# No block, last waits in order of issue, w_phi loaded by features, the gate column by one transpose, x on two queues, a split x block, swapped banks: small edits to a linear-attention and GEGLU kernel

## The chip, the cores and the metric

One core of one Trainium2 chip. The metric is the device time of one execution in microseconds (us). Every profile read here shows the granted TensorE clock at 1.00. "Span" is the time from the first to the last recorded instruction of the core.

## The reference

```python
x = A_x                                            # 1 x 2048 x 640, bf16
g = sigmoid((x * gate_w).sum(-1, keepdims=True))
# A: linear attention, 32 heads of 20; feature map = softmax(+p), softmax(-p) of p = head @ w_phi
# (p enters only through exponentials, so wq @ blockdiag(w_phi) can be folded beforehand; same for wk)
a = attention(x, wqkv, w_phi) @ wo
b = (gelu(x @ w_gate) * (x @ w_up)) @ w_down       # F = 1728
return g * a + (1 - g) * b
```

## The kernel before

The kernel keeps everything in SBUF. It warms TensorE with seven matmuls of zeros, transposes the first 512 tokens of x on TensorE, and computes v for them while the other operands land. A tile of x is 128 tokens, so these are tiles 0 to 3, and a block is four tiles. The other x blocks, wk and wq come through transposing DMAs on SyncE's queue ("turns" below). wk and wq are then multiplied with the block-diagonal w_phi on TensorE ("folds"). From about 16 us on, an almost unbroken stream of matmuls runs to 294 us. Matmuls write into PSUM, which the kernel uses in numbered banks. These are the parts that the change touches:

```python
    def finish(self, eng):                     # last thing in the program, on SyncE
        for q in self.queues.values():
            for L in q["lanes"]:
                if L["count"] > 0:
                    eng.wait_ge(L["sem"], L["count"])
        for e in self.engs.values():
            if e["count"] > 0:
                eng.wait_ge(e["sem"], e["count"])

    def run(self):
        nc = self.nc
        self.alloc()
        with nc.Block() as blk:
            @blk.sync
            def _(sp):
                self.sc = _Sched(nc, {"sp": (nc.sync, 16), "act": (nc.scalar, 4), "pool": (nc.gpsimd, 2)})
                self.loads(); self.attention_state(); self.ffn()      # (three lines, joined here)
                self.sc.finish(sp)
    # ...
    # loads(): w_phi as 20 x 640 and the gate row on ScalarE's queue; on SyncE's queue:
        xload(0); xload(2)                     # tokens 0..511, two halves
        for kt in range(KD): vload(kt)         # wv
        xblock(1)                              # tokens 512..1023 turned: tiles 4 to 7
        wload(self.wkT, D, "wkT")              # wk turned
        wload(self.wqT, 0, "wqT")
        xblock(2); xblock(3)
    # ...
    def blockdiag(self, banks):                # between the v steps of the first block
        # 5 matmuls spread w_phi over the partitions, 5 more turn the gate row into a column,
        # then VectorE multiplies each with a 0/1 mask out of PSUM  (cut)
    # ...
        self.v_early(4, 6)                     # v of tile 4, banks 6 and 7
        self.v_early(5, 0)
        f(0, "k", (2, 3), "d")                 # fold 0 of wk
        f(1, "k", (4, 5), "a")
        self.v_early(6, 6)
    # ...
    # ffn(): PSUM bank pairs for gate and up
        pairs = [(6, 7), (0, 1)]               # the last query projection wrote bank 7
```

The softmax here doesn't subtract the row's maximum and nothing guards it: scores larger than these inputs give would overflow.

## Time and profile before

| | |
|---|---|
| device time, three runs at first | 299.22 us (299.12 to 299.34) |
| device time, all later runs of it (42, in four jobs) | mean 298.75 us (298.20 to 299.72) |
| span, mean of those 42 | 297.02 us |
| span of the profiled execution | 297.3 us |

The page of the profile, its first lines and the engines' shares of the chain of waits. Columns of the engine line: busy us, share of the span, number of instructions.

```profile
span 297.3 us, 4821 instructions
PE 292.5 (98%) x1913; PEld 170.3 (57%) x1913; DVE 162.6 (55%) x322; ACT 104.3 (35%) x183; POOL 28.0 (9%) x56
...
PE 93%; SPq 2%; DMA 2%; ACT 1%; issue 0%; ACTq 0%
```

TensorE does nearly everything, so only its stops and the two ends of the program are left to gain in. This is the timeline of TensorE's matmuls in the first 17 us (start us, duration us, engine, line, operation, tiles, count, and in brackets the idle time before it):

```profile
4.45 2.08 PE L285 MATMUL ps<-ident,xtok 128*128 128x128 bf16 x20
6.36 3.44 PE L369 MATMUL ps<-w,xT 128*128 128x480 bf16 x24
9.73 0.48 PE L305 MATMUL ps<-wphi_sb,esel 20*128 20x140 bf16 x5
10.05 0.26 PE L313 MATMUL ps<-one,gw_row 1*128 1x1 bf16 x5
10.25 2.35 PE L369 MATMUL ps<-w,xT 128*128 128x480 bf16 x16
12.44 2.88 PE L360 MATMUL ps<-w,xT 128*128 128x512 bf16 x20
15.63 0.80 PE L340 MATMUL ps<-BD,wkT 128*128 128x140 bf16 x12 [0.31 <-DMA wkT<-in_A_wqkv_dram]
16.27 1.52 PE L360 MATMUL ps<-w,xT 128*128 128x512 bf16 x10
```

The ten small matmuls take 0.52 us of the queue (9.73 to 10.25). At 15.63 TensorE has waited for the turned wk. From start to start, TensorE stood still 0.48 us (its last matmul started at 15.10 and holds the queue 0.055).

The same view where the feed-forward part begins.

```profile
83.92 1.24 PE L617 MATMUL ps<-xT,wg_sb 128*128 128x512 bf16 x5
85.36 1.24 PE L617 MATMUL ps<-xT,wu_sb 128*128 128x512 bf16 x5 [0.19 <-ACT Eq L511]
```

The end, from the views of single source lines (line, queue, instruction, count: shortest/median/longest ns, first and last start in us). SyncE's waits are L98 and L101, the exit of the block is L130:

```profile
L98 SPq EVENT_SEMAPHORE  x7: 17/28/902, 295.4 to 296.6; - x7
L101 SPq EVENT_SEMAPHORE  x4: 28/28/28, 296.7 to 296.9; - x4
...
L130 SPq COMPARE_BRANCH  x1: 41/41/41, 297.0 to 297.0; - x1
L130 SPq DRAIN  x1: 13/13/13, 297.1 to 297.1; - x1
L130 SPq EVENT_SEMAPHORE  x1: 17/17/17, 297.3 to 297.3; - x1
L130 ACTq EVENT_SEMAPHORE  x1: 17/17/17, 297.3 to 297.3; - x1
L130 DVEq EVENT_SEMAPHORE  x1: 21/21/21, 297.3 to 297.3; - x1
L130 PEldq EVENT_SEMAPHORE  x1: 51/51/51, 297.3 to 297.3; - x1
```

The 902 ns wait is the one for the last output, which landed at 296.47. Everything after it is bookkeeping: 0.88 us.

### The profile page before, as it was taken

Reading aid. Unit: us, or ns where it says so; the run is one execution under the profiler, and the core shown is the slowest. Engines: PE = TensorE matmul, PEld = TensorE weight load, DVE = VectorE, ACT = ScalarE, POOL = GpSimd, SP = SyncE. Lnnn points to the kernel's source line nnn. Section 1 sums busy time; section 2 is a strip of 40 time slices with the busy share of each in tenths; the row PEclk is TensorE's granted clock in tenths of the full one; section 3 lists DMA queues with packets and bytes.
Section 4 is the critical chain, followed back from the end, with each engine's and each line's share of the span. In section 5 each row is a group of like instructions: output and inputs, shape, how many; then the busy total and the mean of one; then the engine's idle time right before and its main releaser. Section 6 shows DMA issues by size and latency. Waiting matters only on the chain.

```text
span 297.3 us, 4821 instructions
## 1 busy us (share of the span) xinstructions
PE 292.5 (98%) x1913; PEld 170.3 (57%) x1913; DVE 162.6 (55%) x322; ACT 104.3 (35%) x183; POOL 28.0 (9%) x56
## 2 busy tenths in 40 slices
PE   8999999999999999999999999999999999999996
PEld 4566566555554455765554567654556765555673
DVE  1338999998876578600777700077770007777100
ACT  3357787666673221112222211222221122222112
POOL 7000000000000011110111100011110001111000
DMA  7999990000001304211011130101111010111101
GB/s 217 203 223 337 356 345 29 0 0 2 0 2 32 57 8 35 49 46 44 3 23 22 24 44 24 44 0 25 22 22 46 22 45 2 22 24 22 44 24 44
DMA packets 38178, 18.85 MB, mean 63 GB/s; under 512 B 30219, under 2 KB 37900, under 8 KB 38156
## 3 DMA queue, kind: packets, MB, share of 16 engines
q1 hardware_dynamic: 37504, 18.52, 24.9%
q8 instruction: 15, 0.25, 0.3%
q10 hardware_dynamic: 652, 0.03, 0.2%
q14 instruction: 7, 0.06, 0.1%
HBM read 9.04 MB, written 2.62 MB: 39 GB/s over the span
## 4 chain that ended last, share of the span: by engine, by line
PE 93%; SPq 2%; DMA 2%; ACT 1%; issue 0%; ACTq 0%
PE ps L617 37%; PE ps L716 19%; PE ps L360 12%; PE ps L722 7%; PE ps L505 7%; PE ps L653 4%; PE ps L453 3%; DMA wkT<-in_A_wqkv_dram 2%; PE ps L627 1%; SPq L229 1%; PE ps L340 1%; PE ps L695 1%; SPq L216 1%; ACT Eq L511 1%; ACT Ek L419 0%
## 5 line engine op out<-in xcount | busy, mean ns | idle before, releaser
L622 DVE TENSOR_TENSOR hT<-ps,gl 128x512 bf16<-128x512 f32 x52 | 35.7, 689 | 80.1 <-PE ps L617 80.0
L617 PE MATMUL ps<-xT,wu_sb 128*128 128x512 bf16 x260 | 64.6, 379 | 0.2 <-ACT Eq L511 0.2
L617 PE MATMUL ps<-xT,wg_sb 128*128 128x512 bf16 x260 | 64.6, 379 | 0.0
L620 ACT ACTIVATE gl<-ps 128x512 bf16<-128x512 f32 x52 | 31.1, 597 | 82.9 <-PE ps L617 80.6
L716 PE MATMUL ps<-wd_sb,hT 128*128 128x320 bf16 (+2 forms) x416 | 59.3, 299 | 0.0
L716 PEld LDWEIGHTS ps<-wd_sb,hT 128*128 128x128 bf16 x416 | 40.2, 98 | 16.8
L682 POOL TENSOR_TENSOR Og<-O,O 128x640 bf16<-128x640 bf16 x16 | 22.3, 1396 | 244.6 <-DVE O L680 244.6
L617 PEld LDWEIGHTS ps<-xT,wu_sb 128*128 128x128 bf16 x260 | 25.4, 98 | 31.1 <-issue 0.7
L360 PE MATMUL ps<-w,xT 128*128 128x512 bf16 (+3 forms) x240 | 40.9, 321 | 0.0
L617 PEld LDWEIGHTS ps<-xT,wg_sb 128*128 128x128 bf16 x260 | 24.9, 98 | 26.5
L732 ACT ACTIVATE outsb<-ps,Gm 128x640 bf16<-128x640 f32 (+2 forms) x17 | 13.0, 763 | 71.5 <-PE ps L722 71.5
L360 PEld LDWEIGHTS ps<-w,xT 128*128 128x128 bf16 x240 | 22.4, 97 | 18.2
L430 DVE TENSOR_REDUCE Dk<-Ek 128x64 f32<-128x1280 bf16 x16 | 23.7, 1481 | 3.2 <-ACT gcol L422 3.2
L439 DVE TENSOR_TENSOR Ek<-Ek,Dk 128x640 bf16<-128x640 bf16 x32 | 25.0, 822 | 0.6
L505 PE MATMUL ps<-xT,wq 128*128 128x512 bf16 x100 | 24.7, 379 | 0.3 <-ACT Eq L511 0.3
L680 DVE TENSOR_TENSOR O<-ps,RH 128x640 bf16<-128x640 f32 x32 | 24.8, 816 | 0.0
L722 PE MATMUL ps<-wo_sb,goT 128*128 128x320 bf16 (+2 forms) x160 | 24.6, 299 | 0.0
L511 ACT ACTIVATE Eq<-ps 128x512 bf16<-128x512 f32 x40 | 21.7, 604 | 4.0 <-PE ps L505 4.0
L419 ACT ACTIVATE Ek<-ps 128x640 bf16<-128x640 f32 x32 | 20.7, 702 | 3.5 <-PE ps L360 3.5
L722 PEld LDWEIGHTS ps<-wo_sb,goT 128*128 128x128 bf16 x160 | 15.1, 98 | 7.2 <-issue 1.3
L653 PEld LDWEIGHTS ps<-KV,Eq 128*128 128x128 bf16 x192 | 12.0, 98 | 3.6
L653 PE MATMUL ps<-KV,Eq 128*128 128x154 bf16 x192 | 13.7, 221 | 0.0
(66 smaller groups left out, 151.4 us busy)
## 6 DMA issues: line engine op xcount, KB each, us to landing
out_dram<-outsb SPq DMA_DIRECT2D x15, 160.0 KB, 1.8
wd_sb<-in_B_w_down_dram SPq DMA_DIRECT2D x1, 2080.0 KB, 12.6
wg_sb<-in_B_w_gate_dram SPq DMA_DIRECT2D x1, 1120.0 KB, 5.7
wu_sb<-in_B_w_up_dram SPq DMA_DIRECT2D x1, 1120.0 KB, 9.5
wg_sb<-in_B_w_gate_dram SPq DMA_DIRECT2D x1, 960.0 KB, 9.8
wu_sb<-in_B_w_up_dram SPq DMA_DIRECT2D x1, 960.0 KB, 10.1
w<-in_A_wqkv_dram SPq DMA_DIRECT2D x5, 160.0 KB, 4.0
wo_sb<-in_A_wo_dram SPq DMA_DIRECT2D x1, 800.0 KB, 9.8
```

The lines of the kernel that those rows point to most:

```text
L360: sc.op("pe", lambda e, kt=kt: e.matmul(self.bank(bank)[:, bcol:bcol + n], self.xT[:, kt, t * P:(t + 1) * P], self.w3[:, kt, c0:c0 + n], s ...
L430: sc.op("dve", lambda e: e.tensor_reduce(self.Dk[:, se, 0, :].rearrange("p (s h) -> p s h", h=H), self.Ek[:, se, :, :].rearrange("p s (h d ...
L439: sc.op("dve", lambda e, v=v, r=r: e.tensor_tensor(v, v, r, ALU.mult), reads=[("Rk", se)], writes=[("Ek", se, s)])
L505: sc.op("pe", lambda e, kt=kt: e.matmul(self.bank(bank), self.wq2[:, kt, i * P:(i + 1) * P], self.xT[:, kt, b * self.BT:(b + 1) * self.BT] ...
L511: sc.op("act", lambda e, s=s, scale=scale: e.activation(self.Eq[:, s, i, b * self.BT:(b + 1) * self.BT], self.bank(bank), AF.Exp, scale=sc ...
L617: sc.op("pe", lambda e, kt=kt, w=w, bk=bk: e.matmul(self.bank(bk), w[:, kt, c * P:(c + 1) * P], xs(kt), start=(kt == 0), stop=(kt == self. ...
L620: sc.op("act", lambda e: e.activation(self.gl[:, slot, :], self.bank(banks[0]), AF.Gelu_apprx_tanh), reads=[("ps", banks[0])], writes=[("g ...
L622: sc.op("dve", lambda e: e.tensor_tensor(self.hT[:, c, :], self.bank(banks[1]), self.gl[:, slot, :], ALU.mult), reads=[("ps", banks[1]), ( ...
L653: sc.op("pe", lambda e, s=s, i=i, n=n, o0=o0, k0=k0, bk=bk, r=r: e.matmul(self.bank(bk)[:, o0:o0 + n], self.Eq[:, s, i, t * P:(t + 1) * P] ...
L680: dve(lambda e, o=o, f=f, s=s: e.tensor_tensor(o, V[s][:, :, :, 0:DH], f, ALU.mult), rb + [key(6 + s)], [("O", s, sl)], guard=old)
L716: sc.op("pe", lambda e: e.matmul(self.bank(bk, w), self.hT[:, c, tt * P:(tt + 1) * P], self.wd_sb[:, c, w0:w0 + w], start=(c == 0 and not ...
L722: sc.op("pe", lambda e: e.matmul(self.bank(bk, w), self.goT[:, gs, k, :], self.wo_sb[:, k, w0:w0 + w], start=False, stop=(k == self.KD - 1 ...
```

## The change

The intent: take the bookkeeping off the end, the ten small matmuls and the two stops off TensorE, and bring wk earlier. The core of the diff, with some lines joined (initialisers, allocations, the later x blocks and the pool engine's selector are cut):

```diff
     def finish(self, eng):
-        for q in self.queues.values(): ...
         for e in self.engs.values():
             if e["count"] > 0:
-                eng.wait_ge(e["sem"], e["count"])
+                self._wait(eng, _Ev(e["sem"], e["count"]))
+        lanes = [L for q in self.queues.values() for L in q["lanes"] if L["count"] > 0]
+        for L in sorted(lanes, key=lambda L: L["last"]):      # in order of issue
+            self._wait(eng, _Ev(L["sem"], L["count"]))
@@ run
-        with nc.Block() as blk:
-            @blk.sync
-            def _(sp): ...
+        self.loads(); self.attention_state(); self.ffn()
+        self.sc.finish(nc.sync)
@@ loads
-        xload(0); xload(2)                    # both on SyncE's queue
+        xload("sp", 0)
+        xload("act", 2)
+        # w_phi as (h d) f -> 128 partitions x 5 x 20 on ScalarE's queue; the gate row into 5 rows of a
+        # zeroed 128 x 128 tile gz
-        xblock(1)
+        xturn(4, 2)
         wload(self.wkT, D, "wkT")
+        xturn(6, 2)
         wload(self.wqT, 0, "wqT")
@@ blockdiag
-        # ten matmuls into PSUM, then five products out of PSUM
+        for i in range(self.KD):              # five products, SBUF to SBUF
+            sc.op("dve", ... BD[:, i] = wphi_sb[:, i, :] (broadcast over heads) * mask[:, i])
+    def gate_column(self, b):
+        sc.op("pe", lambda e: e.transpose(pv, self.gz[:, :], self.ident[:, :]), ...)
+        sc.op("dve", lambda e: e.tensor_copy(self.w3[:, :, 2*D:2*D+1], pv[:, 0:KD].unsqueeze(2)), ...)
@@ attention_state
-        vs(0, 0); vs(1, 0); vs(2, 0); vs(0, 1); vs(3, 0); ...
+        for t in range(4): vs(t, 0)           # plain order
@@ ffn
-        pairs = [(6, 7), (0, 1)]
+        pairs = [(0, 1), (6, 7)]
```

More of the change, by code (lines that the diff above doesn't have):

```diff
@@ L34, in __init__ @@
         self.bufs = {}
+        self.issued = 0
     def _wait(self, eng, ev):
@@ L91, in dma @@
         L["count"] += 16
+        self.issued += 1
+        L["last"] = self.issued
         self._record(reads, writes, (qkey, lane), _Ev(L["sem"], L["count"]))
     def finish(self, eng):
-        for q in self.queues.values():
-            for L in q["lanes"]:
-                if L["count"] > 0:
-                    eng.wait_ge(L["sem"], L["count"])
         for e in self.engs.values():
             if e["count"] > 0:
-                eng.wait_ge(e["sem"], e["count"])
+                self._wait(eng, _Ev(e["sem"], e["count"]))
+        lanes = [L for q in self.queues.values() for L in q["lanes"] if L["count"] > 0]
+        for L in sorted(lanes, key=lambda L: L["last"]):
+            self._wait(eng, _Ev(L["sem"], L["count"]))
 class _Kernel:
@@ L129, in run @@
         self.alloc()
-        with nc.Block() as blk:
-            @blk.sync
-            def _(sp):
-                self.sc = _Sched(nc, {"sp": (nc.sync, 16), "act": (nc.scalar, 4), "pool": (nc.gpsimd, 2)})
-                self.loads()
-                self.attention_state()
-                self.ffn()
-                self.sc.finish(sp)
+        self.sc = _Sched(nc, {"sp": (nc.sync, 16), "act": (nc.scalar, 4), "pool": (nc.gpsimd, 2)})
+        self.loads()
+        self.attention_state()
+        self.ffn()
+        self.sc.finish(nc.sync)
     def alloc(self):
@@ L156, in alloc @@
         self.zero = T("zero", [P, 512], BF16)
-        self.gw_row = T("gw_row", [1, D], BF16)
-        self.one = T("one", [1, 1], BF16)
+        self.gz = T("gz", [P, P], BF16)
         self.gcol = T("gcol", [P, NT], F32)
@@ L163, in alloc @@
         self.BD = T("BD", [P, KD, 8 * DH], BF16)
-        self.wphi_sb = T("wphi_sb", [DH, D], BF16)
-        self.esel = T("esel", [DH, 8, DH], BF16)
+        self.wphi_sb = T("wphi_sb", [P, KD, DH], BF16)
         def place(lists):
@@ L209, in loads, with xload, xturn @@
         x4 = self.x[0:self.BT, :].rearrange("(p j) n -> p j n", j=self.TB)
-        def xload(j):
-            sc.dma("sp", lambda e: e.dma_start(self.xtok[:, j:j + 2, :], x4[:, j:j + 2, :]),
+        def xload(q, j):
+            sc.dma(q, lambda e: e.dma_start(self.xtok[:, j:j + 2, :], x4[:, j:j + 2, :]),
                    writes=[("xtok", j), ("xtok", j + 1)])
-        def vload(kt):
-            sc.dma("sp", lambda e: e.dma_start(self.w3[:, kt, 0:D], w3[:, kt, 2 * D:3 * D]), writes=[("wv", kt)])
-        sc.dma("act", lambda e: e.dma_start(self.wphi_sb[:, :].rearrange("d (h f) -> d h f", f=DH),
-                                            self.wphi.rearrange("h d f -> d h f")), writes=["wphi"])
-        sc.dma("act", lambda e: e.dma_start(self.gw_row[0:1, :], self.gw.rearrange("(o n) -> o n", o=1)), writes=["gw_row"])
-        xload(0)
-        xload(2)
-        for kt in range(KD):
-            vload(kt)
         def wload(T, c0, key):
             sc.dma("sp", lambda e: e.dma_start_transpose(T[:, :, :], self.wqkv[:, c0:c0 + D]), writes=[key])
-        def xblock(b):
-            sc.dma("sp", lambda e: e.dma_start_transpose(
-                self.xT[:, :, b * self.BT:(b + 1) * self.BT], self.x[b * self.BT:(b + 1) * self.BT, :]),
-                writes=[("xT", t) for t in range(b * 4, b * 4 + 4)])
-        xblock(1)
+        def xturn(t, n):
+            a, z = t * P, (t + n) * P
+            sc.dma("sp", lambda e: e.dma_start_transpose(self.xT[:, :, a:z], self.x[a:z, :]),
+                   writes=[("xT", k) for k in range(t, t + n)])
+        sc.op("pool", lambda e: e.memset(self.gz[:, :], 0.0), writes=["gz"])
+        xload("sp", 0)
+        xload("act", 2)
+        sc.dma("act", lambda e: e.dma_start(
+            self.wphi_sb[:, :, :], self.wphi.rearrange("h d f -> (h d) f").rearrange("(i p) f -> p i f", p=P)),
+            writes=["wphi"])
+        for kt in range(KD):
+            sc.dma("sp", lambda e: e.dma_start(self.w3[:, kt, 0:D], w3[:, kt, 2 * D:3 * D]), writes=[("wv", kt)])
+        sc.dma("act", lambda e: e.dma_start(self.gz[0:KD, :], self.gw.rearrange("(k p) -> k p", p=P)), writes=["gz"])
+        xturn(4, 2)
         wload(self.wkT, D, "wkT")
+        xturn(6, 2)
         wload(self.wqT, 0, "wqT")
-        xblock(2)
-        xblock(3)
+        xturn(8, 4)
+        xturn(12, 4)
         half = 7 * P
@@ L258, in loads @@
                                        compare_op=ALU.not_equal, fill=1.0, base=0, channel_multiplier=1), ["ident"])
-        pool(lambda e: e.tensor_copy(
-            self.esel[:, :, :], self.ident[0:DH, 0:DH].unsqueeze(1).to_broadcast([DH, 8, DH])), ["esel"], reads=["ident"])
         for i in range(KD):
@@ L293, in x_transpose @@
             sc.op("dve", lambda e: e.tensor_copy(out, src), reads=[("ps", b)], writes=[("xT", t)])
-    def blockdiag(self, banks):
-        sc = self.sc
-        DH = self.DH
-        es = self.esel[:, :, :].rearrange("d j f -> d (j f)")
-        plan = []
-        for bk, chunks in zip(banks, ((0, 1, 2), (3, 4))):
-            c = 0
-            for r, i in enumerate(chunks):
-                n = (self.HHI[i] - self.HLO[i] + 1) * DH
-                off = (P * i) % DH
-                sc.op("pe", lambda e, i=i, n=n, c=c, off=off, bk=bk, r=r: e.matmul(
-                    self.bank(bk)[:, c:c + n], es[:, off:off + P],
-                    self.wphi_sb[:, self.HLO[i] * DH:self.HLO[i] * DH + n], start=(r == 0), stop=(i in (2, 4)),
-                    skip_group_check=True),
-                    reads=["esel", "wphi"], writes=[("ps", bk)], signal=(i in (2, 4)))
-                plan.append((i, bk, c, n))
-                c += n
-        for kt in range(self.KD):
-            sc.op("pe", lambda e, kt=kt, c=c, bk=bk: e.matmul(
-                self.bank(bk)[:, c + kt:c + kt + 1], self.gw_row[0:1, kt * P:(kt + 1) * P], self.one[:, :],
-                start=False, stop=(kt == self.KD - 1), skip_group_check=True), reads=["gw_row", "one"],
-                writes=[("ps", bk)], signal=(kt == self.KD - 1))
-        for i, b, cc, n in plan:
-            sc.op("dve", lambda e, i=i, b=b, cc=cc, n=n: e.tensor_tensor(
-                self.BD[:, i, 0:n].rearrange("p (h d) -> p h d", d=DH),
-                self.bank(b)[:, cc:cc + n].rearrange("p (h d) -> p h d", d=DH),
-                self.mask[:, i, 0:n // DH].unsqueeze(2).to_broadcast([P, n // DH, DH]), ALU.mult),
-                reads=[("ps", b), ("mask", i)], writes=[("BD", i)])
-        sc.op("dve", lambda e: e.tensor_copy(
-            self.w3[:, :, 2 * self.D:2 * self.D + 1], self.bank(bk)[:, c:c + self.KD].unsqueeze(2)),
-            reads=[("ps", bk)], writes=["wgate"])
@@ new lines, in blockdiag @@
+    def blockdiag(self):
+        DH = self.DH
+        for i in range(self.KD):
+            n = self.HHI[i] - self.HLO[i] + 1
+            self.sc.op("dve", lambda e: e.tensor_tensor(
+                self.BD[:, i, 0:n * DH].rearrange("p (h d) -> p h d", d=DH),
+                self.wphi_sb[:, i, :].unsqueeze(1).to_broadcast([P, n, DH]),
+                self.mask[:, i, 0:n].unsqueeze(2).to_broadcast([P, n, DH]), ALU.mult),
+                reads=["wphi", ("mask", i)], writes=[("BD", i)])
+    def gate_column(self, b):
+        sc = self.sc
+        pv = self.bank(b).bitcast(BF16)[:, 0:P]
+        sc.op("pe", lambda e: e.transpose(pv, self.gz[:, :], self.ident[:, :]),
+              reads=["gz", "ident"], writes=[("ps", b)])
+        sc.op("dve", lambda e: e.tensor_copy(self.w3[:, :, 2 * self.D:2 * self.D + 1], pv[:, 0:self.KD].unsqueeze(2)),
+              reads=[("ps", b)], writes=["wgate"])
@@ L529, in attention_state @@
         sc.op("dve", lambda e: e.memset(self.zero[:, :], 0.0), writes=["zero"])
-        sc.op("dve", lambda e: e.memset(self.one[:, :], 1.0), writes=["one"])
         def warm(n):
@@ L541, in attention_state @@
         xt(3, 3, "a")
-        vs(0, 0)
-        vs(1, 0)
-        vs(2, 0)
-        vs(0, 1)
-        vs(3, 0)
-        vs(1, 1)
-        vs(2, 1)
-        vs(3, 1)
+        for t in range(4):
+            vs(t, 0)
+        for t in range(4):
+            vs(t, 1)
         for t in range(4):
             vs(t, 2)
-        self.blockdiag((6, 7))
         for t in range(4):
             vs(t, 3)
+        self.blockdiag()
+        self.gate_column(6)
         for t in range(4):
```

## The prediction

> **What bounds it now.** TensorE: 98% of the 297.3 us span on the page, clock 1.00, and 93% of the chain of waits. Four small places are left to gain in:
> - Start. Transposes of x start at 4.45 us: the first half of x lands at 4.40 (records of DMA landings), the seven warm-up matmuls end at 4.43.
> - 9.73 to 10.25 (timeline): ten small matmuls that spread w_phi and the gate weights, 0.52 us of TensorE's queue.
> - 15.16 to 15.63: TensorE has issued both early v tiles and waits for the turned wk, landed at 15.59 (waits view: 0.3 us on matmuls, 0.5 on weight loads).
> - 85.18 to 85.36: the first gate/up pair writes the banks of the last query projection and waits 0.2 us for ScalarE's exponentials (waits view).
> - End. The last output lands at 296.47; SyncE then walks seven event waits (0.06 us each) to 296.92 and the block's exit to 297.35: 0.87 us.
>
> **What each part is worth**
> 1. No block, waits in order of issue, engines first: nearly all of that tail goes, -0.8 us, all on the path.
> 2. Gate column by one transpose: 0.52 us of matmuls out, 0.06 to 0.1 in (warm 128-column transposes start 0.056 apart). The five mask products stay on VectorE, from SBUF, while it is idle. -0.43 us of TensorE's queue; it counts only if wk and x come earlier too.
> 3. Halved block around wk: turns move 284 rows of 256 B per 0.25 us (DMA packet records), so 1280 fewer packets ahead bring wk 1.1 us earlier, and the x half moved to ScalarE's queue frees 0.5 us of SyncE's issue. Estimate: wk lands near 13 to 14, no longer binding. But each turn ends in 0.65 to 0.8 us of thin traffic, and there is one more. Tiles 6 and 7 land about 15.0, where TensorE will ask at about 15.3: part may come back as a wait for tile 6. Before, a 16,384-byte instruction packet at 13.25 held one DMA engine 1.17 us, and the wk turn thinned to nothing for about 1 us. The Trainium skill ("Runtime: NRT & Kernel Launch", Instruction fetch mechanics) says that instructions come in 16 KiB blocks by DMA; the trace agrees. This fetch should now fall at about 14, into the second x half. Steps 2 and 3 together: -0.9 us at best, -0.3 with that collision; I take -0.65.
> 4. x on two queues: the Trainium skill ("DMA: Bandwidth & Descriptors", Issuing engines are not separate DMA queues) says that it saves issue time only, as both share the 16 engines. The first half now shares with the second instead of w_phi's 640 packets of 40 B; estimate: 4.3, second half 4.5 instead of 5.38. TensorE starts within 0.15 us of before; the new v order asks for tile 3 about 0.1 us too early. Net 0.
> 5. Banks swapped: -0.18 us.
>
> From 16 to 295 us TensorE's work is the same.
>
> **Predicted: 297.6 us** (299.22 - 0.8 - 0.65 - 0.18), range 297.0 to 298.4. Faster by over 2%: 0.005; within 2%: 0.985; slower by over 2%: 0.01.
>
> **What would show it.** One SyncE wait after the last landing; one transpose for ten matmuls; wk landing before 14.5 with no TensorE wait for it; tile 6 landing at 15 to 16; no gap at the first gate/up pair; stages from 90 us on equally long.
>
> **What would make it wrong.** x landing later on two queues; the clock rising later than 6.02, as transposes before it run at half speed; the extra turn making tile 6 over 0.6 us late; a barrier at program end as dear as the block's.

## The result, and the profile after

| | before | after |
|---|---|---|
| device time, median of six | 299.02 us | 296.28 us (295.87 to 297.35) |
| ratio, with its 95% interval | | 0.9918 (0.9898 to 0.9937) |
| device time, mean of the runs with a span (42 and 21) | 298.75 us | 296.34 us |
| span, mean of these runs | 297.02 us | 295.10 us |
| device time minus span | 1.73 us | 1.24 us |
| from the start of the last matmul to the end of the span (profiles) | 2.97 us | 2.13 to 2.14 us |

A ratio here and below is the mean time of one kernel's fast runs over that of the other's fast runs of the same rounds, so it is not quite the ratio of the medians. The gain is 2.4 to 2.7 us; the prediction was 1.6. The measured time lies below the predicted range.

The page:

```profile
span 296.1 us, 4789 instructions
PE 291.0 (98%) x1904; PEld 169.1 (57%) x1904; DVE 162.7 (55%) x321; ACT 104.2 (35%) x183; POOL 27.8 (9%) x56
...
PE 93%; SPq 3%; DMA 2%; ACT 1%; issue 0%; ACTq 0%
```

This profile fell on the slowest of the first six executions of the kernel after (297.35, span 296.1; the other five have spans of 294.6 to 295.7). TensorE's timeline says why:

```profile
4.47 1.29 PE L280 MATMUL ps<-ident,xtok 128*128 128x128 bf16 x20 [0.24 <-DMA xtok<-in_A_x_dram]
5.60 4.72 PE L350 MATMUL ps<-w,xT 128*128 128x480 bf16 x32
10.16 0.22 PE L303 MATMUL ps<-ident,gz 128*128 128x128 bf16 x1
10.22 1.25 PE L350 MATMUL ps<-w,xT 128*128 128x480 bf16 x8
11.30 2.88 PE L341 MATMUL ps<-w,xT 128*128 128x512 bf16 x20
14.02 0.79 PE L321 MATMUL ps<-BD,wkT 128*128 128x140 bf16 x12
16.20 1.53 PE L341 MATMUL ps<-w,xT 128*128 128x512 bf16 x10 [1.39 <-DMA xT<-in_A_x_dram]
```

Three things are to be seen. One transpose (10.16 to 10.22) stands where ten matmuls were. The first fold starts at once at 14.02, as wk landed at 13.38. And the time so won is lost again to tile 6 of x, which landed at 16.16: the matmul behind the folds starts at 16.20, only 0.07 us earlier than its like in the kernel before.

The twenty transposes took 1.29 us here and 2.08 in the profile of before. That is no part of the change. They start 0.107 us apart while TensorE runs at half speed and 0.056 apart after its clock has risen, and the moment of the rise differs between executions of one kernel. The Trainium skill, "TensorE: Matmul & The Clock Gate", What's actually happening, says that the clock is released by a free-running window of activity, so that the number of slow matmuls varies from run to run; the traces agree (0, 20, 19 and 10 of the 20 transposes were slow in four profiles of the kernel after). The profile's own clock column says 1.00 throughout and does not show it. The clock record in the packed traces does where there is one: its stretch at full clock begins at 3.90 us in this profile, and at 6.63 and 5.85 in those with 19 and 10 slow transposes.

At the start of the feed-forward part the stop is gone (0.216 us from the fifth gate matmul at 84.729 to the first up matmul at 84.945):

```profile
83.87 1.24 PE L594 MATMUL ps<-xT,wg_sb 128*128 128x512 bf16 x5
84.94 1.24 PE L594 MATMUL ps<-xT,wu_sb 128*128 128x512 bf16 x5
```

And at the end, from the view of the source line of SyncE's waits between 294 and 297 us, the last wait is the last instruction of the program:

```profile
L42 SPq EVENT_SEMAPHORE  x10: 17/28/28, 295.0 to 296.1; - x10
```

From 95 us to the last matmul the two traces run in step, 0.41 us apart all the way: 0.35 from the bank stop and 0.06 from the front of this slow execution.

### The profile page after: what moved, and what is told of

The parts are those of the page before. It is cut to its first block, busy times and chain, and to the rows that moved or that the text cites. A ratio compares the mean times of both kernels' runs of the same rounds, so it can differ in the third digit from the quotient of the medians.

```text
span 296.1 us, 4789 instructions
## 1 busy us (share of the span) xinstructions
PE 291.0 (98%) x1904; PEld 169.1 (57%) x1904; DVE 162.7 (55%) x321; ACT 104.2 (35%) x183; POOL 27.8 (9%) x56
## 4 chain that ended last, share of the span: by engine, by line
PE 93%; SPq 3%; DMA 2%; ACT 1%; issue 0%; ACTq 0%
PE ps L594 38%; PE ps L693 19%; PE ps L341 12%; PE ps L699 8%; PE ps L486 7%; PE ps L630 4%; PE ps L434 3%; DMA xT<-in_A_x_dram 2%; SPq L213 2%; PE ps L604 1%; PE ps L672 1%; PE ps L321 1%; SPq L217 1%; SPq L226 1%; ACT Ek L400 0%; ACT Eq L492 0%
## 5 line engine op out<-in xcount | busy, mean ns | idle before, releaser
L597 ACT ACTIVATE gl<-ps 128x512 bf16<-128x512 f32 x52 | 31.1, 597 | 82.5 <-PE ps L594 80.3
L630 PE MATMUL ps<-KV,Eq 128*128 128x154 bf16 x192 | 13.7, 221 | 0.0
## 6 DMA issues: line engine op xcount, KB each, us to landing
wd_sb<-in_B_w_down_dram SPq DMA_DIRECT2D x1, 2080.0 KB, 13.7
```

The costliest lines, as they stand in the source:

```text
L597: sc.op("act", lambda e: e.activation(self.gl[:, slot, :], self.bank(banks[0]), AF.Gelu_apprx_tanh), reads=[("ps", banks[0])], writes=[("g ...
L630: sc.op("pe", lambda e, s=s, i=i, n=n, o0=o0, k0=k0, bk=bk, r=r: e.matmul(self.bank(bk)[:, o0:o0 + n], self.Eq[:, s, i, t * P:(t + 1) * P] ...
```

## The experiments

All kernels gave correct results. Each ran with the kernel before on the same chip; five rounds, unless said.

### 1. The kernel after again, on three chips

No edit. Kernels `after_again`, `after_third` and `after_fourth`.

> The kernel after, unchanged, in five rounds and with a second profile. In the profile on record TensorE waited 1.4 us for tile 6 of x (landed at 16.16 us), and that run was the slowest of six (297.35 against a median of 296.28). Theory A (the late tile is a collision of the second x half with an instruction fetch, and depends on how TensorE and the queue happen to stand to each other): typical runs have a span near 295.0, and in their profile tile 6 lands before 15.3 or TensorE waits for it under 0.5 us. Rival B (the wait is there in every run, the slow one has lost time elsewhere): the wait for tile 6 is again over 1 us although the span is 295. In both, the time minus the span is 1.25 us, 0.5 less than in the kernel before.

> The kernel after, unchanged, as the reference on this chip and for a third profile. Seven profiles of kernels with the split so far have tile 6 landing between 13.7 and 16.2 us and TensorE asking for it between 14.7 and 15.9, earlier the sooner its clock rises. Expected: median 296.2 to 296.6, time minus span 1.26, tile 6 somewhere in that range.

> The kernel after, unchanged, as the reference on this chip. Expected: median 296.2 to 296.6, time minus span 1.24 to 1.26 us.

Measured: medians 296.25, 296.38 and 295.80 us; ratios 0.9919 (0.9905 to 0.9932), 0.9919 (0.9906 to 0.9933) and 0.9909 (0.9892 to 0.9925). Time minus span is 1.26, 1.23 and 1.24 us. The last median, 295.80, lies below what was expected of it. The table puts together what the profiles say of the front; landings are from the records of DMA landings, "asked" is the end of the work ahead on TensorE's queue, all in us. (`no_split`, `x_one_queue` and the others are described below.)

| profile of | slow transposes, of 20 | tiles 4, 5 land | wk lands | tiles 6, 7 land | tile 6 asked | stop for it |
|---|---|---|---|---|---|---|
| after | 0 | 9.86 | 13.38 | 16.16 | 14.65 | 1.56 |
| after_again | 20 | 10.02 | 13.42 | 15.83 | 15.80 | 0.07 |
| after_third | 19 | 8.47 | 12.10 | 13.97 | 15.65 | none |
| after_fourth | 10 | 8.46 | 11.73 | 13.68 | 15.40 | none |
| x_one_queue_2 | 16 | 10.23 | 13.99 | 16.84 | 15.21 | 1.68 |
| before | 15 | 11.10 (block) | 15.59 | 11.10 | wk: 15.16 | 0.48 (wk) |
| before_no_block | 7 | 10.20 (block) | 14.54 | 10.20 | wk: 14.86 | none |
| no_split | 16 | 11.02 (block) | 14.56 | 11.02 | wk: 14.65 | none |

What follows: the late tile is not in every execution, so rival B falls. Over the nine profiles that share this front (these four, block_back, old_banks and the three hold kernels below) the stop for tile 6 was 1.56 us in the profile on record, 0.77 us in block_back and at most 0.08 us in the others.

Theory A's cause for it, a collision with an instruction fetch, is at most a part. In the profile on record a 16,384-byte instruction packet did run at 14.05, inside the second half's turn, as predicted. Over the eleven profiles with this split and order of v (the nine and the two of experiment 7), such a packet fell between the landings of wk and of tile 6 in five, and these five have the latest tile 6 (15.32 to 16.84 us; 13.65 to 15.17 in the six others). From wk's landing to tile 6's it took 2.40 to 2.85 us in the five and 1.65 to 2.29 in the six. That is a coincidence seen, not an isolated cause. And the wk turn of the profile on record was already 1.3 us later than in `after_third`, with no fetch near it: there the traffic thinned to almost nothing between 8.75 and 9.75, with single packets of 256 B taking over 1 us where 18 ns are usual. So the same turn lands up to 2.5 us apart from one execution to another, and only part of that coincides with fetches. What makes the long packets stays open.

### 2. The block

```diff
 # block_back: the kernel after, with
+        with nc.Block() as blk:
+            @blk.sync
+            def _(sp):  (body and finish as before)
 # before_no_block: the kernel before, with
-        with nc.Block() as blk: ...
```

> The kernel after with the block put back around its body; the new order of the last waits stays. Theory A (the block cost its exit inside the span and another 0.5 us outside it, which is why the gain was more than predicted): the span grows by about 0.4 us (branch, drain, barrier, release after the last wait), the time minus the span goes back from 1.25 to about 1.8, total +0.9 us. Rival B (the 0.5 us outside the span comes from the other queues and waits): +0.4 us only, time minus span stays at 1.25.

> The kernel before with nothing changed but the block taken away (its old order of last waits stays). Theory A: span -0.4 us, time minus span down from 1.8 to 1.25, total -0.9 us against before. Rival B (the time outside the span is not the block's): -0.4 us in all. Everything ahead of 295 us unchanged but for the moment at which the TensorE clock rises, which may differ between executions by up to 3 us and is worth up to 0.8 us (16 half-speed transposes in the profile of before).

Measured on one chip: block_back 297.90 us median, ratio to before 0.9969 (0.9956 to 0.9982), against 0.9919 for the kernel after. before_no_block 297.73 us, ratio 0.9969 (0.9955 to 0.9983). By means, putting the block back costs 1.51 us, and taking it away alone gains 0.93. Of that, in the profiles, 0.36 to 0.44 us lies between the last matmul and the end of the span. Time minus span goes from 1.26 to 1.95 with the block back, and from 1.75 to 1.44 with it taken away: a difference of 0.3 to 0.7 us that no recorded instruction accounts for. So the block costs more than its visible exit. How much more depends on the kernel around it, and the fall to 1.25 that was expected of before_no_block did not come: 0.2 us stayed. A remaining 0.4 and 0.3 us lie ahead of the last matmul, where the block has no instruction; with a scatter of 1 us per execution I cannot tell it from chance (block_back's profile had the late tile 6), and it stays open.

The new order of the last waits is the other part of the tail. With the block in both, the tail shrank from 2.97 (before) to 2.57 us (block_back), and without it from 2.61 (before_no_block) to 2.13 (after): 0.40 and 0.48 us.

### 3. Whose end costs time outside the span

```diff
 # hold_engines: the kernel after, behind finish()
+        end = max(lanes, key=lambda L: L["last"])           # lane of the last output
+        for e in (nc.tensor, nc.vector, nc.scalar, nc.gpsimd):
+            e.wait_ge(end["sem"], end["count"])
 # hold_tensor: (nc.tensor,) only;  hold_three: (nc.vector, nc.scalar, nc.gpsimd) only; three rounds each
```

> The kernel after, with one more wait at the end of the TensorE, VectorE, ScalarE and GpSimd streams for the last output's landing, as the block's exit held them. No block. Theory A (the time outside the span shrank because without the block four engines end their streams early and only SyncE is left at the end): time minus span rises from 1.26 to 1.6 to 1.9 us; the span grows by at most 0.1. Rival B (it is the block's own branches and instructions): time minus span stays at 1.26.

> The kernel after with only TensorE's stream held until the last output has landed. Theory A (whatever each engine has to do after its stream is long for TensorE alone): time minus span about 1.8 us, as when all four were held. Rival B (it is the other engines'): 1.25 us. Rival C (each adds something): in between.

> The kernel after with VectorE's, ScalarE's and GpSimd's streams held until the last output has landed, TensorE's not. Theory A (TensorE alone): time minus span 1.25 us. Rival B (the others): about 1.8 us. Rival C: in between.

Measured: the span hardly moves (mean 295.28 with all four held; 295.10 for the kernel after), but the time does. The view of the added line in hold_engines shows that each wait ends at once when the last output has landed:

```profile
L140 ACTq EVENT_SEMAPHORE  x1: 17/17/17, 295.3 to 295.3; - x1
L140 POOLq EVENT_SEMAPHORE  x1: 17/17/17, 295.4 to 295.4; - x1
L140 DVEq EVENT_SEMAPHORE  x1: 21/21/21, 295.4 to 295.4; - x1
L140 PEldq EVENT_SEMAPHORE  x1: 51/51/51, 295.4 to 295.4; - x1
```

| kernel | time minus span | ratio to before |
|---|---|---|
| after (21 runs) | 1.24 us | 0.9909 to 0.9919 |
| hold_tensor (4) | 1.47 us | 0.9919 (0.9903 to 0.9935) |
| hold_three (4) | 1.84 us | 0.9943 (0.9925 to 0.9961) |
| hold_engines (5) | 1.79 us | 0.9947 (0.9935 to 0.9959) |
| before (42 runs) | 1.73 us | |

Four semaphore waits that no block is needed for bring back 0.55 us, so theory A holds: what counts is that the engines' streams end late, not the block's own instructions. Holding the other three costs all of it. Holding TensorE alone costs 0.23 us, but ten_matmuls below, which holds no stream, shows 0.2 us more as well, so that share is not sure (by the numbers, hold_tensor is rival C and hold_three rival B). The Trainium skill, "Runtime: NRT & Kernel Launch", The ~15µs preamble/postamble breakdown, lists steps that follow a kernel, among them a barrier that waits for all engines and then a reset of each engine's semaphores. If each engine did what comes before such a barrier as soon as its own stream ends, an engine that ends early would have done it while SyncE still waits for the output. That would fit, but no trace here shows those steps, so why a late end costs this time is not shown.

### 4. The banks of the first gate/up pair

```diff
-        pairs = [(0, 1), (6, 7)]
+        pairs = [(6, 7), (0, 1)]
```

> The kernel after with the first gate/up pair on banks 6 and 7 again. Read from the starts of matmuls (not from their modelled ends, as I did in the prediction), TensorE stood still 0.35 us there (84.789 + 0.216 to 85.355). Theory A: the time grows by 0.35 us and the same gap of some 0.57 us between two starts comes back at the first gate/up pair. Rival B (the prediction's size, 0.18 us): +0.18. Both small against the scatter of single executions, so the profile's gap decides, not the time.

Measured: 296.75 us median, ratio 0.9932 (0.9916 to 0.9947), against 0.9909 to 0.9919 for the kernel after. (That ran on other chips; so here, in experiment 5 and for tile6_later the comparison goes over the kernel before, which ran on each.) The stop is back in the timeline, with 0.57 us between the starts of the fifth gate matmul and the first up matmul, where 0.216 would do:

```profile
83.05 1.24 PE L594 MATMUL ps<-xT,wg_sb 128*128 128x512 bf16 x5
84.48 1.24 PE L594 MATMUL ps<-xT,wu_sb 128*128 128x512 bf16 x5 [0.19 <-ACT Eq L492]
```

So the swap is worth 0.35 us by the profile, not the 0.18 that I took from the bracket. The times cannot decide it: their intervals overlap.

### 5. The ten matmuls

The kernel after with the old blockdiag(), selector, and loads of w_phi and the gate row.

```diff
-        self.blockdiag()
-        self.gate_column(6)
+        self.blockdiag((6, 7))
```

> The kernel after with the ten small matmuls, the selector and the old loads of w_phi and gate weights back in place of the one transpose. Theory A (the front is bound by TensorE in typical executions): +0.43 us. Rival B (it is bound by the landing of tile 6): within 0.15 us, TensorE only waits less for tile 6.

Measured: 297.04 us median, ratio 0.9949 (0.9935 to 0.9962). By means the span grows by 0.55 us (295.65) and the time minus span by 0.2 (1.46). The first is theory A: the front of a typical execution is bound by TensorE's own work. The timeline shows the 0.52 us again, and no wait behind it:

```profile
11.20 0.48 PE L302 MATMUL ps<-wphi_sb,esel 20*128 20x140 bf16 x5
11.53 0.26 PE L310 MATMUL ps<-one,gw_row 1*128 1x1 bf16 x5
11.72 1.26 PE L366 MATMUL ps<-w,xT 128*128 128x480 bf16 x8
```

The kernel after did not run on this chip; hold_engines, which equals it up to the last output, did, with a mean span of 295.28. Against that the ten matmuls cost 0.37 us of span, near the 0.43 expected. The 0.2 us outside the span I had not expected and cannot explain. It is the same 0.2 us that stayed in before_no_block, which has the old loads and the ten matmuls too.

### 6. The split of the x block

```diff
-        xturn(4, 2)
+        xturn(4, 4)
         wload(self.wkT, D, "wkT")
-        xturn(6, 2)
```

> The kernel after with the second x block turned in one piece ahead of wk, as before. Theory A (split and wk order are worth something): wk lands near 14.6 to 15.6 where TensorE asks at about 14.0, so a wait of 0.6 to 1.6 us for wk appears in place of the one for tile 6; time 0.3 to 0.7 us above the kernel after. Rival B (the extra turn costs as much as the order saves): within 0.2 us of the kernel after, or faster.

Measured on one chip with after_again: 296.51 us against 296.25, ratio 0.9924 (0.9910 to 0.9937) against 0.9919. That is rival B: the split by itself is worth nothing that these runs can tell. wk landed at 14.56, just ahead of TensorE:

```profile
11.93 2.88 PE L340 MATMUL ps<-w,xT 128*128 128x512 bf16 x20
14.65 0.79 PE L320 MATMUL ps<-BD,wkT 128*128 128x140 bf16 x12
```

In the kernel before, the turns began 0.6 us later, behind the second x load (4.21 against 3.62), and in its profile wk was late, at 15.59. But before_no_block has the same loads, and there wk landed at 14.54 without a stop. So the late wk that the split was meant to cure was not in every execution either.

### 7. x on one queue

```diff
-        xload("act", 2)
+        xload("sp", 2)
```

> The kernel after with both x halves issued by SyncE again. Theory A (two queues save issue time only, worth nothing at the start and 0.47 us of a turn that is not always the limit): first half lands 3.8 to 4.2 instead of 4.4, second half near 4.8, every turn lands up to 0.5 us later, time within 0.3 us of the kernel after. Rival B (two queues bring x earlier): transposes start later than 4.6, +0.3 us or more.

> x_one_queue once more, as its first result (297.0 against 296.44 for the kernel after, five and four runs) was too scattered to decide, and its profile showed no wait that would explain it. Theory A (worth nothing; the scatter is the moment of the clock's rise): within 0.25 us of the kernel after. Rival B (two queues are worth 0.3 us or more): again 0.3 to 0.6 us slower.

Measured: 296.93 us and 297.24 us median; ratios 0.9938 (0.9924 to 0.9953) where the kernel after had 0.9919, and 0.9949 (0.9933 to 0.9965) where it had 0.9909 (0.9892 to 0.9925). The second pair of intervals does not overlap. By means it is 0.6 and 1.2 us slower. So two queues are worth something, although they do not bring the first half of x earlier: on one queue it landed at 3.99 and 3.88 us, on two at 4.43, 4.43, 4.49 and 4.66 (the second half at 5.12 and 5.02 against 4.62 to 4.93). What they bring is SyncE's issue time: on one queue the first turn is issued at 4.10 us, on two at 3.62 to 3.65. The second profile shows what can follow (waits view of the first 30 us: what waited for what, us in total, times, longest):

```profile
PEld ps L341 <- DMA xT<-in_A_x_dram: 1.7, 1, 1.7
PE ps L341 <- DMA xT<-in_A_x_dram: 1.5, 1, 1.5
```

Tile 6 landed at 16.84. The first profile of the same kernel has no such wait (tile 6 at 15.17), so here too it would be a matter of how often it happens, which two profiles cannot tell. That this wait makes up the 0.6 and 1.2 us is not shown. The Trainium skill, "DMA: Bandwidth & Descriptors", Issuing engines are not separate DMA queues, says that issuing from several engines saves only the sequencer's time, "which is usually small relative to the DMA itself". The landings of x agree with the first half of that. The saving of 0.47 us of issue was not small here, if it is what made the difference: the turns behind it on the queue were due just in time.

### 8. Orders of TensorE's work that should make the landings harmless

```diff
 # tile6_later: the kernel after, v of tile 6 behind four folds instead of two
-        self.v_early(6, 6)          # behind fold 1
+        self.v_early(6, 2)          # behind fold 3 (folds 2 and 3 on banks 6,7 and 0,1)
 # whole_v6_first: no_split, and this (the banks of folds 2 to 4 and of tile 7, moved with it, are cut)
+        self.v_early(6, 6)          # ahead of fold 0
 # better: whole_v6_first, and the third and fourth query projections on other banks
-        self.pq(0, 3, 3)
+        self.pq(0, 3, 3, 0)
-        self.pq(0, 2, 2)
+        self.pq(0, 2, 2, 7)
```

> The kernel after with tile 6's v projection moved behind four folds of wk instead of two, so it is asked for 0.64 us later; same matmuls, same loads. Theory A (the late second half costs something in every execution): faster than the kernel after by 0.3 to 0.6 us, and in the profile the wait for tile 6 shrinks by 0.6. Rival B (typical executions, 0.9 us faster than the profiled ones, never wait for tile 6): within 0.15 us of the kernel after, or slower if the folds now wait for their evacuations.

> The kernel after with the x block turned whole ahead of wk, and tile 6's v projection put ahead of the first fold instead of behind two of them, so that nothing that TensorE asks for lands late: x block near 11, wk near 14.6 where it is now asked for at 15.4 to 16.2. Theory A (the split bought room that the order of TensorE's work gives for nothing): no wait for x or wk in the profile, time equal to the kernel after or 0.2 to 0.4 us lower, spread set by the clock's rise alone. Rival B (the split matters of itself): slower than the kernel after by 0.3 us or more, with a wait for wk.

> The same, with the third and fourth query projections of the first block sent to banks 0 and 7. In every profile so far TensorE stands still 0.5 us at the third one (0.72 between two starts instead of 0.216), since its bank still holds the first one's values until ScalarE has taken the exponentials. Expected: that gap gone, -0.5 us against whole_v6_first. Rival: ScalarE is the limit there and the gap moves to the next projection; then -0.1 or less.

Measured: tile6_later 296.85 us, ratio 0.9935 (0.9922 to 0.9948); whole_v6_first 296.67, 0.9921 (0.9907 to 0.9935); better 296.58, 0.9924 (0.9910 to 0.9937), where the kernel after had 0.9919. None beats it. In seven of the nine profiles named in experiment 1 TensorE hardly waited for tile 6, so there was little to save. The spread that is left goes with the moment of the clock's rise: the first gate matmul started at 82.3 to 82.5 us in the three profiles with at most 2 slow transposes and no late tile (tile6_later, better, hold_tensor), and at 83.0 to 83.6 in the six of the kernel after, old_banks and the hold kernels that had 10 or more and no late tile. In better the stop at the third projection is gone, but TensorE now stops at the products behind it, for VectorE's normalised features (waits view, 20 to 60 us):

```profile
PEld ps L433 <- DVE Ek L419: 0.8, 2, 0.5
PE ps L433 <- DVE Ek L419: 0.2, 1, 0.2
```

From the first query projection to the first gate matmul it took 56.86 us in better and 56.89 in whole_v6_first. The stop had not been the limit; VectorE stood behind it.

## Why the prediction was wrong

It gave 297.6 us; the mean of all 21 runs is 296.34. Set against the measured terms:

| term | predicted | measured |
|---|---|---|
| base | 299.22 | 298.75 (42 runs) |
| step 1, tail inside the span | -0.8 | -0.84 (2.97 to 2.13) |
| outside the span | not in it | -0.49 (1.73 to 1.24; the block alone -0.31 in the old kernel, 0.69 when put back in the new one) |
| step 5, banks | -0.18 | -0.35 |
| steps 2, 3 and 4, front | -0.65 | -0.73 (the rest of the mean difference, 2.41) |

- **The step that failed is step 1**: "No block, waits in order of issue, engines first: nearly all of that tail goes, -0.8 us". The mechanism and the visible part were right. But I took the recorded span for the whole time and did not ask what the 1.7 us beyond it hold. There 0.49 us went as well. Holding the other engines' streams to the end brings back 0.55 (hold_engines), and the block 0.69 (block_back). Taking the block alone from the kernel before gave 0.31; the last 0.2 us goes with the old loads and the ten matmuls (ten_matmuls), and its cause stays open.
- **Step 5 was mis-sized** by a factor of two. The idle time in the bracket is counted from a modelled end; the stop on the queue is the distance of the starts less the matmul's own 0.216 us.
- **The base** was three runs of one session that lay 0.47 us above the mean of 42; the next three of that session were lower (298.41 to 298.93). With a single-execution scatter of 1 us and a forecast gain of 1.6, a range of 297.0 to 298.4 around it was too narrow.
- **The front was right in sum, and wrong in its parts.** Step 2 held: the ten matmuls are worth their queue time (0.37 to 0.55 us of span). Step 3 named a collision in the second half of x and found it in the profile on record, but it is not typical, and the split itself is worth nothing measurable. Step 4, "Net 0", was booked for the start alone; two queues were worth 0.6 and 1.2 us in two comparisons. The issue time that they free, which I had booked under step 3, is the likely reason, but not a shown one. These parts do not add up to the measured front, since each was taken out of a kernel that had the others.
- "Stages from 90 us on equally long" and "one SyncE wait after the last landing" held. The new order of the v steps did ask for tiles of x too early, as step 4 said: 0.13 and 0.04 us of stops, from start to start, in the profile on record.

## What to carry to other kernels

Compare the device time with the span before costing the end of a program: work that keeps idle engines' streams open to the end (a block's exit barrier, a last wait on each engine) can be paid again after the last recorded instruction, here with 0.3 to 0.7 us. Size a stop of TensorE by the distance between the starts of matmuls, not by idle time against modelled ends. When single executions scatter by as much as the effect in question, one profile shows what can happen, not what usually does; read several.

## What the Trainium skill lacked or had wrong

- "Runtime: NRT & Kernel Launch" does not say what it costs to keep the streams of idle engines open to the end: holding four engines' streams cost 0.55 us outside the span (1.24 to 1.79).
- "TensorE: Matmul & The Clock Gate" gives the moment of the clock's rise as varying by 500 ns either way. Here it varied more: in four profiles of one kernel, all with the first matmul at about 1.26 us, 0, 10, 19 and 20 of the 20 transposes between about 4.5 and 6.6 us ran at half speed (0.107 us apart instead of 0.056), and the clock records put the rise at 3.90, 5.85 and 6.63 us in the first three. No page says that the profile's granted clock stays at 1.00 through it.
- "DMA: Bandwidth & Descriptors" says that saving a sequencer's issue time "is usually small relative to the DMA itself". Moving one issue of 0.47 us off the queue was worth 0.6 and 1.2 us here in two comparisons; that the issue time is the reason is likely, as the turns behind it were due just in time, but not shown.
- No page gives the cost of one DMA transpose behind another on one queue. Here the traffic thins towards the end of a turn (in the profile on record from some 284 packets of 256 B per 0.25 us to between 68 and 124 for 1.0 us from 12.0 us on), and the same turn landed up to 2.5 us apart in different executions (tiles 6 and 7 at 13.7 to 16.2 in four profiles of the kernel after).
- "Runtime: NRT & Kernel Launch", Instruction fetch mechanics, calls the fetch of a 16 KiB block mostly hidden. Each such packet kept a DMA engine busy for 0.88 to 1.76 us in the profiles of the kernel after. In eleven profiles the five with such a packet between the landings of wk and of tile 6 have the latest tile 6, but no run here isolates its cost.
